# Other periods for the sums, steps and loads of one kv batch in a pipelined attention and adapter kernel

## The chip, the cores and the metric

The kernel runs on one core of one Trainium2 chip. The metric is the device time of an execution in microseconds (us). Before the change it is 384.3 us, the median of 3 runs (384.18 to 384.46).

## The reference

Four batches of 12288 query tokens attend to a pooled and projected image, and the result goes through a mixture of eight small adapters, of which each token uses two. Cut to what is computed:

```python
# q (4, 12288, 128), kv (4, 384, 32, 128), w_sr (128, 128)
kv_pool = kv.reshape(B, H // 4, 4, W // 4, 4, C).mean(axis=(2, 4))
k = v = kv_pool.reshape(B, -1, C) @ w_sr          # 768 keys a batch
a = softmax(q @ k.T / sqrt(C))
x = a @ v                                         # 49152 tokens in all
logits = x @ w_gate                               # 8 experts
topk = the two largest logits of a token; w = softmax over these two
out = x + sum over the two experts e of w_e * ((x @ A[e]) @ B[e])   # rank 16
```

## The kernel before, in words

The 49152 tokens are 96 chunks of 512, 24 to a batch. A hand-written main loop runs over c = 2 to 94, and I call one pass a period. All engines run their instructions in the order in which this loop records them; nothing reorders them. In one period TensorE does, in this order: two groups of scores (L303, keys against queries, each group two matmuls into one of two score banks), with the first half of the weighing of chunk c-1 (L315, values against exps) between them; from c=10 on the up projection of an older chunk (L462); the second half of the weighing; a kv step if one is due in this period (prep_step); the turn of the normalised x of chunk c-2 (t_ps, L381); a third group of scores; and from c=9 on the hidden matmul of an older chunk (L416). At the end of the periods 6 and 8 a further group of scores is recorded, so that scores run a little further ahead.

ScalarE takes the exp of each score group (L304), and in odd periods, between the second and the third exp, the tanh of the gates of a pair of chunks (L358). It also copies the results of the kv steps out of the score banks (L191, L199, L207). VectorE normalises (L322, L326), finds the largest logits (L333), and does the other evacuations. GpSimd computes the arguments of the gates for a pair of chunks in even periods (gate, L342 to L346, behind VectorE's L333), casts the next queries to f16 (cast_q, L107), and sums the kv rows. SyncE issues the loads, the turns of the queries by DMA (L114), the transport of the gates (L402, L409) and the stores.

While the loop works on one batch, the keys and values of the next are prepared. A batch has three tiles of kv, each loaded in four rows of 512 KB (load_row, L87). sum_row (L173) adds row d to row 0 on GpSimd, three times a tile, and after the third sum_cols (L177, L178) halves the row twice. Then TensorE has three steps a tile, in three periods: pooled_transposed (kp_ps, L189) in period k, values (v_ps, L197) in k+2, keys (k_ps, L205) in k+3. Each writes to a score bank that ScalarE copies out. The keys of the second batch are first used by the scores at the end of c=22.

When this happens stands in three lists in plan(b): `at` gives the periods of the 12 loads, `sm` those of the 9 row sums, `st` those of the three first steps. For the second batch, b=1, the numbers are periods themselves; for later batches they are relative to the period at which the batch before begins. prep, called near the end of each period behind gate and cast_q, issues the loads and the sums that are due; so in an even period a sum stands behind that period's gate and cast, and in an odd one it follows what is there. prep_step records a step between the weighing and the turn of x.

In the periods 17, 19 and 21 GpSimd also squares the values (squares, L241 and L245), for a check of ranges.

Of the kernel before, what the change touches and what calls it, by code (L numbers as in the profile page):

```python
# [21 lines left out]
def kernel(  # L22
# [232 lines left out]
    def plan(b):  # L255
        c0 = CPB * (b - 1)
        if b == 1:
            at = [2, 2, 3, 4, 5, 6, 6, 8, 9, 10, 10, 12]
            sm = [5, 5, 7, 9, 9, 11, 13, 13, 15]
            st = [10, 14, 18]  # L260
        else:
            at = [-11, -9, -7, -5, -5, -3, -1, 1, 1, 3, 5, 7]
            sm = [-3, -1, 1, 3, 5, 7, 9, 11, 13]
            st = [4, 10, 16]
        for i, k in enumerate(at):
            loads.setdefault(c0 + k, []).append((b, i // 4, i % 4))
        for i, k in enumerate(sm):
            sums.setdefault(c0 + k, []).append((b, i // 3, i % 3 + 1))
        for t, k in enumerate(st):
            steps[c0 + k] = (pooled_transposed, b, t)  # L270
            steps[c0 + k + 2] = (values, b, t)
            steps[c0 + k + 3] = (keys, b, t)

    for b in range(1, B):
        plan(b)
# [729 lines left out]
```

## Time and profile before

| | us |
|---|---|
| median of 3 runs | 384.3 |
| lowest, highest | 384.18, 384.46 |
| the profiled execution | 383.93 |
| its span in the profile | 382.1 |
| TensorE busy in the span | 363.3 |
| ScalarE busy | 311.4 |
| VectorE busy | 305.2 |
| GpSimd busy | 224.0 |

The span is the time between the first and the last recorded instruction; the execution's own time is 1.83 us longer. Busy times come from that one execution. PE is TensorE's matmuls, PEld its weight loads, DVE is VectorE, ACT ScalarE, POOL GpSimd, SP SyncE. In a timeline row the first number is the start in us, the second the length of the group, and a bracket at the end gives idle time before it with what ended it. Matmuls are pipelined and the lengths of neighbouring groups overlap, so the pace is read from starts.

### The profile page before, as it was taken

To read this page: it belongs to the slowest core of one execution; us is meant where nothing else is said; L and a number is where in the kernel's file an instruction comes from. 1 tells how busy PE (TensorE), PEld (TensorE's weight loads), DVE (VectorE), ACT (ScalarE), POOL (GpSimd) and SP (SyncE) were. 2 spreads that over 40 slices of the span, in tenths; PEclk is the share of its full clock that TensorE was granted. 3 is DMA by queue.
4 is the path that set the end of the run, shared out by engine and by line. 5 is a ranking of instruction groups with operands and counts; after the bars stand their busy time and mean duration, and the time that the engine had idled before them with its cause. 6 is when DMAs were issued, how large, how long until landed. Compare 5 with 4: busy or idle time off the path is not lost.

```text
span 382.1 us, 10633 instructions
## 1 busy us (share of the span) xinstructions
PE 363.3 (95%) x3962; PEld 268.5 (70%) x3963; DVE 305.2 (80%) x955; ACT 311.4 (82%) x393; POOL 224.0 (59%) x369
## 2 busy tenths in 40 slices
PE   4889999999999999999999999999999999999983
PEld 2457667777777877777777777777776777776772
DVE  3786538787888888888888888888888888889995
ACT  1548998889888988988898899888798798888752
POOL 1012699996889787755679697754443243341253
PEclk9999999999999999999999999999999999999996
DMA  8996999999999999999999999996997898964225
GB/s 254 405 352 193 262 308 235 340 251 330 343 300 320 311 257 320 270 325 296 314 306 307 294 283 329 289 227 183 238 254 224 255 226 194 239 171 146 88 84 195
DMA packets 93466, 100.48 MB, mean 263 GB/s; under 512 B 56676, under 2 KB 56932, under 8 KB 93412
## 3 DMA queue, kind: packets, MB, share of 16 engines
q1 hardware_dynamic: 91940, 99.58, 94.9%
q8 instruction: 31, 0.51, 0.6%
q10 hardware_dynamic: 1472, 0.20, 0.3%
q14 instruction: 23, 0.19, 0.1%
HBM read 62.33 MB, written 25.90 MB: 231 GB/s over the span
## 4 chain that ended last, share of the span: by engine, by line
PE 73%; POOL 10%; DVE 7%; ACT 5%; issue 2%; DMA 2%; SPq 0%; POOLq 0%; DVEq 0%
PE xps L315 29%; PE sg L303 26%; PE d_ps L462 5%; PE t_ps L381 4%; PE h_ps L416 4%; POOL kvt L173 4%; ACT tt L304 4%; DMA kvt<-in_kv_dram 2%; POOL q L107 1%; DVE xn L326 1%; POOL kvt L177 1%; DVE ht L419 1%; PE v_ps L197 1%; POOL msk L345 1%; PE w_ps L584 1%
## 5 line engine op out<-in xcount | busy, mean ns | idle before, releaser
L304 ACT ACTIVATE tt<-sg 128x1024 f16<-128x1024 f32 x288 | 277.5, 1022 | 36.0 <-PE sg L303 35.1
L303 PE MATMUL sg<-qT,kfT 128*128 128x512 f16 x576 | 170.0, 379 | 2.4 <-ACT tt L304 1.6
L315 PEld LDWEIGHTS <-tt 128*128 128x128 f16 x2304 | 148.0, 98 | 27.0 <-DVE xn L326 17.2
L315 PE MATMUL xps<-vext,tt 128*128 128x137 f16 x2256 | 166.3, 223 | 0.0
L476 DVE TENSOR_TENSOR osb<-d_ps,xn 128x512 f32<-128x512 f32 x88 | 60.6, 691 | 32.3 <-PE d_ps L462 32.1
L342 POOL TENSOR_TENSOR arg<-xn,top 128x64 f32<-128x64 f32 x47 | 14.7, 312 | 109.2 <-DVE top L333 93.2
L326 DVE TENSOR_TENSOR xn<-xps,rinv_all 128x548 f32<-128x548 f32 x94 | 68.5, 728 | 3.3
L303 PEld LDWEIGHTS <-kfT 128*128 128x128 f16 x576 | 49.3, 98 | 26.9 <-issue 3.8
L173 POOL TENSOR_TENSOR kvt<-kvt 128x1024 f32<-128x1024 f32 x27 | 63.7, 2359 | 0.2
L419 DVE SCALAR_TENSOR_TENSOR ht<-ge,h_ps 128x512 bf16<-128x512 f16 x90 | 60.5, 672 | 2.9 <-PE h_ps L416 2.4
L107 POOL CAST q<-q 128x1024 f16<-128x1024 f32 x44 | 45.6, 1036 | 24.9 <-DMA q<-in_q_dram 24.9
L462 PEld LDWEIGHTS <-ht 128*128 128x128 bf16 x368 | 27.3, 97 | 24.7 <-DVE ht L419 3.7
L333 DVE MAX8 top<-xn 128x8 f32<-128x8 f32 x376 | 35.2, 156 | 6.3
L392 DVE COPY xt<-t_ps 128x512 bf16<-128x512 bf16 x92 | 36.7, 399 | 0.0
L381 PE MATMUL t_ps<-id_bf,xn 128*128 128x128 bf16 x376 | 36.3, 219 | 0.0
L416 PE MATMUL h_ps<-xt,a_bf 128*128 128x512 bf16 x89 | 33.7, 379 | 1.0 <-ACT tt L304 0.7
L462 PE MATMUL d_ps<-b_bf,ht 128*128 128x128 bf16 x352 | 33.6, 219 | 0.9 <-ACT tt L304 0.7
L322 DVE RECIPROCAL rinv_all<-xps 128x4 f32<-128x4 f32 x94 | 17.1, 182 | 15.4 <-PE xps L315 13.1
L381 PEld LDWEIGHTS <-xn 128*128 128x128 bf16 x376 | 26.0, 98 | 0.3
L345 POOL TENSOR_SCALAR msk<-msk 128x64 f32<-128x64 f32 x47 | 20.1, 428 | 4.1
L346 POOL TENSOR_TENSOR arg<-arg,msk 128x64 f32<-128x64 f32 x47 | 15.0, 319 | 3.9
L344 POOL TENSOR_TENSOR arg<-arg,msk 128x64 f32<-128x64 f32 x47 | 15.0, 319 | 3.7
(151 smaller groups left out, 228.4 us busy)
## 6 DMA issues: line engine op xcount, KB each, us to landing
kvt<-in_kv_dram SPq DMA_DIRECT2D x48, 512.0 KB
q<-in_q_dram SPq DMA_DIRECT2D x44, 512.0 KB
out_dram<-osb SPq DMA_DIRECT2D x44, 512.0 KB
ge<-g_h SPq DMA_DIRECT2D x45, 256.0 KB
q<-in_q_dram SPq DMA_DIRECT2D x2, 1024.0 KB
out_dram<-osb SPq DMA_DIRECT2D x8, 256.0 KB
g_h<-g_sb SPq DMA_DIRECT2D x45, 16.0 KB
qT<-q SPq DMA_TRANSPOSE x44
```

Of the source, the lines that this page charges most:

```text
L107: nc.gpsimd.tensor_copy(q16[i], q32[i].rearrange("p k n -> p (k n)"))
L173: eng.tensor_tensor(v[:, 0], v[:, 0], v[:, d], op=ALU.add)
L303: mm(sg[:, k], kfT[b][:, j * P:(j + 1) * P], qc, start=True, stop=True)
L304: nc.scalar.activation(tt[c][:, 2 * r:2 * r + 2], sg, AF.Exp, bias=0.0, scale=scale)
L315: mm(o, tt[c][:, j, s * P:(s + 1) * P], vext[b][:, j, 0:VW], start=(j == 0 and s % 2 == 0), stop=(j == NJ - 1 and s % 2 == 1), skip_group_ ...
L326: nc.vector.tensor_tensor(xn[c].rearrange("p (b s) v -> p b s v", b=2), xv, ri.rearrange("p (b s) -> p b s", b=2).unsqueeze(3).broadcast_t ...
L381: mm(columns(t_ps, c, s), src[:, s], id_bf, is_transpose=True, start=(s == 0), stop=(s == NS - 1), skip_group_check=True)
L392: nc.vector.tensor_copy(to, t_ps)
L416: mm(h_ps, a_bf, xT[c], start=True, stop=True)
L419: nc.vector.scalar_tensor_tensor(hgT[c].rearrange("p (k a) t -> p k (a t)", k=2), gE[c // 2][:, h:h + NS // 2].rearrange("p a t k -> p k ( ...
L462: mm(dps[c][:, s], columns(hgT[c], c, s), b_bf, start=(s == 0 and fresh), stop=(s == NS - 1), skip_group_check=True)
L476: nc.vector.tensor_tensor(osb[:, lo:hi], d, xn[c][:, lo:hi, 0:C], op=ALU.add)
```

## The change

Only the lists for the second batch change, and with them the places of 12 loads, 9 row sums, 3 pairs of column sums and 9 steps. The lists of the later batches stay as they are.

```diff
         if b == 1:
-            at = [2, 2, 3, 4, 5, 6, 6, 8, 9, 10, 10, 12]
-            sm = [5, 5, 7, 9, 9, 11, 13, 13, 15]
-            st = [10, 14, 18]
+            at = [2, 2, 3, 4, 5, 5, 6, 8, 9, 9, 11, 13]
+            sm = [3, 5, 6, 8, 9, 10, 12, 14, 16]
+            st = [9, 13, 18]
```

By tile, the sums go from the periods 5, 5, 7 to 3, 5, 6, from 9, 9, 11 to 8, 9, 10 and from 13, 13, 15 to 12, 14, 16, the column sums with the last of each three. The steps pooled, values and keys go from 10, 12, 13 to 9, 11, 12, from 14, 16, 17 to 13, 15, 16, and stay at 18, 20, 21 for the third tile. Four loads move: the second row of the second tile from 6 to 5, and of the third tile the second row from 10 to 9, the third from 10 to 11 and the fourth from 12 to 13.

## The prediction

> **What bounds the kernel now.** Periods are numbered by the loop variable c. Each holds one t_ps group on TensorE (the turn of x, L381), so I use its start as the mark of a period; it is 61.35 us for c=10 and 91.47 us for c=18. I read first the page's chain of work that ended last, then GpSimd's timeline, then TensorE stage by stage between those marks, then what ScalarE waited for. The page:
>
> ```profile
> span 382.1 us, 10633 instructions
> ...
> PE 73%; POOL 10%; DVE 7%; ACT 5%; issue 2%; DMA 2%; SPq 0%; POOLq 0%; DVEq 0%
> ...
> L173 POOL TENSOR_TENSOR kvt<-kvt 128x1024 f32<-128x1024 f32 x27 | 63.7, 2359 | 0.2
> ```
>
> TensorE owns 73% of the chain, but GpSimd owns a tenth, and the kv sums (L173, 2.36 us each, with 0.2 us of waiting before all 27 of them) are in it. The chain's pieces of GpSimd lie between 41.5 and 88 us, in the plan that is changed. GpSimd's timeline there (start, length):
>
> ```profile
> 44.35 4.78 POOL L173 TENSOR_TENSOR kvt<-kvt 128x1024 f32<-128x1024 f32 x2
> 49.10 0.30 POOL L342 TENSOR_TENSOR arg<-xn,top 128x64 f32<-128x64 f32 x1
> ...
> 50.66 0.32 POOL L346 TENSOR_TENSOR arg<-arg,msk 128x64 f32<-128x64 f32 x1
> ...
> 55.70 0.72 POOL L178 TENSOR_TENSOR kvt<-kvt 128x256 f32<-128x256 f32 x1
> 56.39 0.31 POOL L342 TENSOR_TENSOR arg<-xn,top 128x64 f32<-128x64 f32 x1
> ...
> 65.55 0.32 POOL L346 TENSOR_TENSOR arg<-arg,msk 128x64 f32<-128x64 f32 x1
> ...
> 86.18 0.30 POOL L342 TENSOR_TENSOR arg<-xn,top 128x64 f32<-128x64 f32 x1
> ...
> 89.00 1.24 POOL L241 TENSOR_TENSOR sq<-vext 128x272 f32<-128x272 f16 x2
> 92.95 0.31 POOL L342 TENSOR_TENSOR arg<-xn,top 128x64 f32<-128x64 f32 x1 [2.71 <-DVE top L333]
> ```
>
> From 44.35 us to the gate at 86.18 us (c=16) there is no idle time in these rows: a gate takes over as the last sum ends (55.70 + 0.72 is 56.42, the gate starts at 56.39). At 92.95 us (c=18) GpSimd waits for VectorE again, as it should. Two lengths serve below: gate start to gate end is 50.66 + 0.32 - 49.10 = 1.88 us, and gate start over cast, one sum and both column sums is 56.42 - 49.10 = **7.32 us**.
>
> What this lateness costs is read on TensorE, mark to mark (us, then PE, PEld, DVE, ACT, POOL busy, clock, DMA share, GB/s):
>
> ```profile
> 57.73:61.35 3.62, 3.57 (x43) 2.78 (x42) 3.01 (x11) 3.60 (x5) 3.54 (x4) 1.00 0.81 248
> 61.35:64.75 3.40, 3.40 (x42) 2.57 (x39) 2.70 (x9) 3.05 (x5) 3.24 (x5) 1.00 1.21 330
> 64.75:69.07 4.32, 4.07 (x46) 3.10 (x44) 3.44 (x13) 3.40 (x5) 4.15 (x5) 1.00 1.04 242
> 69.07:72.58 3.51, 3.51 (x43) 2.68 (x41) 2.66 (x8) 3.05 (x4) 3.19 (x7) 1.00 1.05 396
> 72.58:76.59 4.01, 3.83 (x44) 2.81 (x42) 3.07 (x12) 3.55 (x6) 3.85 (x5) 1.00 1.25 269
> ...
> 83.96:87.47 3.51, 3.51 (x43) 2.68 (x41) 2.66 (x8) 3.05 (x4) 3.19 (x7) 1.00 0.87 287
> 87.47:91.47 4.00, 3.83 (x44) 2.81 (x42) 3.06 (x12) 3.54 (x6) 2.69 (x5) 1.00 1.27 283
> 91.47:94.87 3.40, 3.40 (x41) 2.56 (x39) 2.71 (x9) 3.05 (x5) 1.67 (x6) 1.00 1.00 340
> ```
>
> A period without a kv step is 3.40 us. The steps lie just ahead of t_ps, and TensorE's timeline gives their start, and the marks 83.96, 87.47 and 91.47 above their end:
>
> ```profile
> 83.45 0.68 PE L197 MATMUL v_ps<-wext,kp_keep 128*128 128x136 f32 x4
> ...
> 87.36 0.28 PE L205 MATMUL k_ps<-id_h,vext 128*128 128x128 f16 x2
> ...
> 91.25 0.38 PE L189 MATMUL kp_ps<-id_f,kvt 128*128 128x128 f32 x2
> ```
>
> Values (L197) cost 0.51, keys 0.11, the pooled turn 0.22 us. So the excess over work is 4.32 - 3.40 - 0.51 = 0.41 (c=12), 4.01 - 3.62 = 0.39 (c=14) and 4.00 - 3.62 = 0.38 us (c=18): **1.18 us**, and nothing in the other rows. Its cause is on ScalarE, in its timeline and its waits from 33 to 110 us:
>
> ```profile
> 65.91 0.32 ACT L358 ACTIVATE gw_all<-arg 128x64 f16<-128x64 f32 x1 [0.82 <-DVE xn L326]
> ```
>
> ```profile
> ACT gw_all L358 <- POOL arg L346: 2.0, 5, 0.5
> ```
>
> The tanh at 65.91 follows GpSimd's row 65.55 + 0.32 = 65.87 directly, so that wait is GpSimd's too (the label is the view's guess). ScalarE would have taken this tanh at 65.91 - 0.82 = 65.09, 3.74 us after its gate's mark 61.35. It stands in line ahead of the exps and of the key copy, and TensorE waits for those.
>
> Behind 91.47 us TensorE alone sets the pace (its busy row, then all it waited for in these 253 us):
>
> ```profile
> 91.47:345.00 253.53, 252.39 (x2852) 189.29 (x2850) 215.25 (x694) 220.92 (x272) 159.36 (x263) 1.00 1.04 273
> ```
>
> ```profile
> PE h_ps L416 <- ACT tt L304: 0.7, 3, 0.2
> PE d_ps L462 <- ACT tt L304: 0.5, 2, 0.2
> ```
>
> So whatever this plan gains or loses by c=18 stands in the total, one for one: there is no later wait to swallow it.
>
> **The change part by part.** No instruction is added or removed; twelve loads, nine row sums with their column sums, and nine steps move. VectorE's order is the same.
>
> *Sums.* One 2.36 us sum goes to c=3, ahead of the stretch without idle time, and the third tile's last sum with its columns goes from 15 to 16. GpSimd has no gate in odd periods, so the sums of 8 and 9 still follow each other without a gate between, as 9 and 9 did. A gate is on time when it ends by 3.74 us behind its mark, so when it starts by 3.74 - 1.88 = 1.86 us behind it. That of c=10 started at 65.87 - 1.88 = 63.99, 0.8 too late; with 2.36 us less ahead it starts with its data. What VectorE needs is in the rows of c=18: weighing done at 91.25, gate at 92.95, 1.70 us.
>
> *Loads.* A sum at c=3 is safe if its two loads (issued in c=2) have landed by about 38.2 us:
>
> ```profile
> 37.00:38.00 1.00, 1.00 (x9) 0.31 (x6) 0.93 (x3) 0.97 (x3) 1.00 (x2) 1.00 0.00 0
> ...
> 39.00:43.00 4.00, 4.00 (x49) 2.96 (x48) 1.61 (x7) 3.77 (x5) 1.32 (x4) 1.00 1.04 288
> ```
>
> ```profile
> 38.69 0.53 SPq L87 DMA_DIRECT2D kvt<-in_kv_dram  x1
> ```
>
> The DMA is silent from 37 to 38, so they have. The tightest is then the load of c=3 (38.69), needed at 44.35: 5.7 us. Ahead of it stand one q load and itself, 1.05 MB, and 4 us at 288 GB/s carry 1.15 MB, so it lands about 43. The others have two to three periods. SyncE's queue gets one issue more (0.5 to 0.7 us) ahead of the gates' transfers in 5, 9 and 13; these are used periods later. I take nothing. If a load were late, GpSimd's gate and cast queued behind the sum would be late as well, by at most what the load lacks; that falls inside the slow end below.
>
> *Steps 9, 11, 12.* The pooled turn comes in c=9, where ScalarE is still behind from the extra score issued at c=8. Its timeline shows the copy that goes with a pooled turn:
>
> ```profile
> 61.55 0.38 ACT L191 ACTIVATE kp_keep<-kp_ps 128x256 f32<-128x256 f32 x1
> ```
>
> In c=9 it could push the exps, so it costs between 0 and 0.4; I take 0: the step brings 0.22 us of TensorE's own, and the tanh in line ahead of the copy is no longer held up.
>
> *The walk.* Mark of 9: 57.73 + 0.22 = 57.95. 10: + 3.40 = 61.35. 11 (values): + 3.91 = 65.26. 12 (keys): + 3.51 = 68.77. 13 (pooled): + 3.62 = 72.39. 14: 75.79. 15 (values): 79.70. 16 (keys): 83.21. The gates keep up: that of 10 at 61.35 + 1.70 = 63.05, then 7.32 us with sum and columns to 70.37, in time for c=12 (68.77 + 1.86 = 70.63); behind 12 and 14 stands one sum each, and GpSimd idles. Then two bare periods: TensorE stands at the third pooled turn of c=18 at 83.21 + 6.80 = **90.01 us**. Before, it stood there at 91.25 us. The 0.41 and 0.39 are gone by here (keys now fall on even periods, where no tanh is), and 0.38 with them; that would be a gain of 1.2 us.
>
> *The third tile.* That turn reads the tile that GpSimd sums in c=16. GpSimd's order there is gate, cast, sum, two column sums, with nothing to take out. Its gate starts 1.70 us after the weighing ends, so at 83.21 - 0.11 + 1.70 = 84.80, and the columns end 7.32 us later, at **92.12 us**. From a mark to the turn two periods on TensorE needs 6.80 us, GpSimd about 8.9. Before, the sum stood in c=15, right behind the gate of 14, and the turn at 91.25 found it done at about 86.2. Now TensorE waits 92.12 - 90.01 = 2.11 us. Queued behind it are the turn of x, the third score, the hidden matmul, and through them ScalarE's exps. The squares behind the columns (1.24 us) and the gate of 18 fall inside this wait. From here the orders are the same, so the end is late by 92.12 - 91.25 = **+0.9 us**: 2.1 lost, 1.2 won.
>
> The profiled execution took 383.93 us for a span of 382.1; it would be 384.8. Beside the median of the runs, 384.3, that is 385.2.
>
> Ends: if none of the 0.80 us ahead of c=16 is won, everything there is 0.8 later and the loss is 1.7; with the copy of c=9 alone, 1.3; if the tanh waits that left no excess on TensorE win 0.3 as well, 0.6. The forecast's own range is 384.9 to 386.0.
>
> **The rivals.**
>
> *The clock falls in the wait.* The trace has one case of a wait like this one, on TensorE near the end:
>
> ```profile
> 375.20 0.40 PE L762 MATMUL e<-id_bf,hgs 128*128 128x128 bf16 x4 [1.92 <-DVE hgs L753]
> ```
>
> ```profile
> 374.00:376.00 2.00, 0.80 (x7) 0.81 (x8) 1.83 (x6) 1.51 (x4) 0.90 (x2) 0.87 0.59 227
> 376.00:378.00 2.00, 2.00 (x17) 1.48 (x16) 0.85 (x3) 0.91 (x3) 1.09 (x4) 0.50 0.68 262
> ```
>
> After 1.92 us of waiting the granted clock went to 0.50. What a cold start costs is in the warming matmuls:
>
> ```profile
> 6.04 6.12 PE L584 MATMUL w_ps<-id_bf 128*128 128x512 bf16 x18 [0.26 <-DVE vext L168]
> ...
> 19.13 1.89 PE L584 MATMUL w_ps<-id_bf 128*128 128x512 bf16 x8
> ```
>
> Eight warm ones take 1.89 us, so 18 would take 4.25 at most, and the first 18 took 6.12: 1.9 us lost. That gives 385.2 + 1.9 = 387.1. Against it: at 375 other short waits came first, here TensorE is full on both sides. The Trainium skill (TensorE: Matmul & The Clock Gate, "Why this matters for your kernels") asks for no gap over some 3 us between bursts; by that rule 2.1 us leave the clock alone and the time is the forecast's. The row at 375.20 shows a fall after less, so I don't rest on it.
>
> *A larger gain ahead of it.* TensorE waited at both extra scores:
>
> ```profile
> 47.98 0.59 PE L303 MATMUL sg<-qT,kfT 128*128 128x512 f16 x2 [0.66 <-ACT tt L304]
> 55.43 0.59 PE L303 MATMUL sg<-qT,kfT 128*128 128x512 f16 x2 [0.72 <-ACT tt L304]
> ```
>
> I hold these for the cost of two extra exps through two score banks. If they too came from late gates, 1.38 us more is won, ahead of c=16: 385.2 - 1.4 = 383.8, within 0.2%. Against: only one tanh before them waited, and the exps around them run back to back.
>
> *The wait does not bind.* If the columns of c=16 end by 90.0 us, TensorE never waits and only the 1.2 us gain is left: 384.3 - 1.2 = **383.1**. It decides at GpSimd's chain: 7.32 us would have to be 5.2, or the two periods 8.9 us long. For it: spans on GpSimd are rough, and no wait of TensorE for GpSimd stands in the trace of before. Against: gate to gate, that chain repeats to within 0.1 us.
>
> *It does not do what it says* would be a first sum held up by its load; the silent DMA speaks against it, and its time lies on the slow side of the forecast's range.
>
> **How the numbers follow.** A difference under 0.2% (0.77 us) can't be told from no change here. Forecast 385.2 us: chance 0.60, of which 0.44 over 385.07 and 0.16 under. Clock: 0.14, slower. Larger gain: 0.11, same. No wait: 0.15, faster. So slower 0.58, same 0.27, faster 0.15. The range of 383.7 to 387.3 us holds all but the last rival and a little at its ends.
>
> **What would show it.** Right: TensorE's turn of the third tile (L189) at c=18 preceded by about 2 us of waiting for L178 on GpSimd; no tanh (L358) waiting for L346 between 55 and 88 us; periods of 3.40 plus their step from 10 to 17. Wrong: that turn without a wait; the waits of 0.66 and 0.72 gone; the clock under 1 at 92 us; GpSimd waiting for a load ahead of a sum.

## The result, and the profile after

The changed kernel takes **386.71 us** (median of 6 executions, 385.02 to 387.28) against 384.06 for the kernel before in the same comparison (383.33 to 384.46): 1.006 times as long, with an interval of 1.0035 to 1.0086. Two of the six lie at 385.0 to 385.1 us, the profiled one (385.12, span 383.3) among them; four lie at 386.4 to 387.3. Two further sets of twelve have medians of 386.24 and 385.82 against 384.11 and 384.17. So the profile after shows a loss of 1.2 us, and the medians of the three sets lie 1.7 to 2.7 us above those of the kernel before. Both have to be explained. The kernel before has a spread too: its 99 executions beside the experiments below reach from 383.37 to 387.96 us.

The page of the profile after:

```profile
span 383.3 us, 10632 instructions
...
PE 82%; DVE 6%; ACT 5%; POOL 2%; DMA 2%; issue 1%; SPq 0%; DVEq 0%; POOLq 0%; ACTq 0%
```

GpSimd's share of the chain fell from 10% to 2%: the lateness that the change was to lift is lifted, and the time still grew. TensorE from mark to mark (the start of t_ps, as in the prediction), periods 10 to 19:

```profile
58.11:61.68 3.57, 3.51 (x41) 2.61 (x39) 2.80 (x10) 3.37 (x6) 3.49 (x3) 1.00 1.22 238
61.68:65.59 3.91, 3.91 (x46) 3.06 (x44) 3.35 (x12) 3.40 (x5) 3.23 (x7) 1.00 1.03 397
65.59:69.10 3.51, 3.51 (x43) 2.68 (x41) 2.71 (x9) 3.08 (x5) 3.43 (x3) 1.00 1.17 239
69.10:72.77 3.67, 3.67 (x44) 2.82 (x42) 2.98 (x11) 3.35 (x5) 3.34 (x8) 1.00 1.05 383
72.77:76.17 3.40, 3.40 (x41) 2.57 (x39) 2.80 (x10) 3.15 (x6) 3.10 (x2) 1.00 1.27 182
76.17:80.08 3.91, 3.91 (x46) 3.07 (x44) 3.34 (x12) 3.39 (x5) 1.97 (x6) 1.00 1.05 403
80.08:83.59 3.51, 3.51 (x43) 2.68 (x41) 2.71 (x9) 3.08 (x5) 2.98 (x2) 1.00 1.61 211
83.59:87.04 3.45, 3.45 (x42) 2.60 (x40) 2.78 (x10) 3.12 (x5) 1.61 (x6) 1.00 0.78 255
87.04:92.85 5.81, 3.84 (x45) 2.82 (x43) 4.45 (x17) 3.43 (x5) 5.65 (x6) 1.00 1.18 293
92.85:96.24 3.39, 3.39 (x41) 2.56 (x39) 1.54 (x3) 2.92 (x4) 3.14 (x8) 1.00 1.04 402
```

Where before there were 4.32, 4.01 and 4.00 us, every period up to 17 is now its bare 3.40 plus its step, to within 0.17 us. Then one period takes 5.81. TensorE's timeline and GpSimd's show why:

```profile
92.57 0.44 PE L189 MATMUL kp_ps<-id_f,kvt 128*128 128x128 f32 x2 [1.97 <-POOL kvt L178]
92.85 0.39 PE L381 MATMUL t_ps<-id_bf,xn 128*128 128x128 bf16 x4
```

```profile
85.18 0.31 POOL L342 TENSOR_TENSOR arg<-xn,top 128x64 f32<-128x64 f32 x1 [2.12 <-DVE top L333]
...
88.01 2.36 POOL L173 TENSOR_TENSOR kvt<-kvt 128x1024 f32<-128x1024 f32 x1
...
91.80 0.72 POOL L178 TENSOR_TENSOR kvt<-kvt 128x256 f32<-128x256 f32 x1
92.47 1.24 POOL L241 TENSOR_TENSOR sq<-vext 128x272 f32<-128x272 f16 x2
```

The gate of c=16 is on time (GpSimd even waits 2.12 us for it), the columns end 91.80 + 0.72 - 85.18 = 7.34 us later, and TensorE has been waiting at the third pooled turn for 1.97 us.

Executions begin up to 1.4 us apart (the mark of c=8 lies between 53.18 and 54.58 us in the traces of this study), so traces are compared below from the mark of c=8 to that of c=25. Before it is 62.59 us, after 63.81: **+1.22**. The two rows:

```profile
53.44:116.03 62.59, 61.22 (x687) 46.21 (x686) 48.83 (x159) 55.23 (x70) 54.44 (x78) 1.00 1.12 301
```

```profile
53.60:117.41 63.81, 61.06 (x686) 46.23 (x685) 48.87 (x159) 55.02 (x70) 53.25 (x77) 1.00 1.10 306
```

### The profile page after: what moved, and what is told of

It reads as the page before. It is cut to its first block, busy times and chain, and to the rows that moved or that the text cites. A ratio compares the mean times of both kernels' runs of the same rounds, so it can differ in the third digit from the quotient of the medians.

```text
span 383.3 us, 10632 instructions
## 1 busy us (share of the span) xinstructions
PE 362.2 (94%) x3962; PEld 268.0 (70%) x3963; DVE 305.1 (80%) x955; ACT 311.4 (81%) x393; POOL 224.2 (58%) x369
## 4 chain that ended last, share of the span: by engine, by line
PE 82%; DVE 6%; ACT 5%; POOL 2%; DMA 2%; issue 1%; SPq 0%; DVEq 0%; POOLq 0%; ACTq 0%
PE xps L315 33%; PE sg L303 29%; PE d_ps L462 5%; PE t_ps L381 5%; PE h_ps L416 4%; ACT tt L304 4%; DMA kvt<-in_kv_dram 2%; PE v_ps L197 1%; DVE xn L326 1%; DVE ht L419 1%; PE w_ps L584 1%; DVE osb L476 1%; DVE kvt L173 1%; POOL kvt L173 1%; PE kp_ps L189 1%
```

## The experiments

The theory: (a) the earlier sums and steps of the first two tiles win about 1 us, (b) the wait of TensorE for the third tile's column sums costs 2 us in every execution, (c) in part of the executions the granted clock falls behind that wait and costs about 2 us more. Rivals: another moved piece makes the loss (loads, squares); the spread comes from somewhere else. In the expectations, "slow group" means the longer ones among the executions of one kernel. The ratios are to the kernel before, run beside each set of four rows: 384.11 us (first four), 384.08 (second four) and 384.17 us (last four). The last column is taken from one trace each.

| kernel | median us | lowest, highest | ratio, 95% | mark 8 to 25, us |
|---|---|---|---|---|
| changed, again | 386.24 | 384.93, 389.19 | 1.0022 to 1.0078 | 65.48 |
| steps at 19 | 384.14 | 383.22, 385.08 | 0.9967 to 1.0008 | 62.96 |
| before, last sum at 16 | 385.27 | 384.63, 386.71 | 0.9997 to 1.0041 | 63.94 |
| sum ahead of the cast | 384.70 | 383.84, 388.05 | 0.9976 to 1.0034 | 62.82 |
| steps at 17 | 391.36 | 390.91, 391.81 | 1.0155 to 1.0216 | 69.13 |
| idle matmuls in the wait | 385.09 | 384.26, 386.23 | 1.001 to 1.0042 | 63.79 |
| sums at 13 and 15 | 384.20 | 383.14, 385.61 | 0.998 to 1.0014 | 62.19 |
| before, new loads only | 385.18 | 383.79, 386.64 | 1.0006 to 1.0042 | 63.15 |
| changed, beside the next three | 385.82 | 384.46, 387.14 | 1.0009 to 1.0054 | 63.80 |
| idle matmuls, beside | 385.65 | 384.85, 387.39 | 1.0017 to 1.0056 | 63.79 |
| sums at 13, 15, loads at 10, 12 | **383.06** | 382.28, 383.89 | 0.995 to 0.9986 | 61.63 |
| steps at 19, squares later | 384.90 | 384.07, 385.66 | 0.9999 to 1.0034 | 61.82 |

**The changed kernel once more** (no edit).

> The changed kernel once more, for its spread and a second trace. Its six executions so far lie in two groups, 385.0 to 385.1 us (the profiled one among them) and 386.4 to 387.3 us; the kernel before lies between 383.3 and 384.5. Theory: the 2 us wait of TensorE ahead of the third pooled turn (L189, c=18) costs about 1 us net in every execution, and in most of them the granted clock falls to 0.5 behind that wait and costs about 2 us more. Then the runs show both groups again, and a trace of the slow group shows a clock of 0.5 for some 3 us just behind 92.6 us and the same period lengths as before elsewhere. Rival: the slow group comes from somewhere else (the end of the kernel, a late transfer); then a slow trace has full clock at 92 us and its loss at another place.

This trace is of one of the longer executions, 386.51 us. The wait at the third turn is the same (1.98 us), but behind it the next period takes 97.92 - 92.86 = 5.06 us where it took 3.39. Its stages, with the granted clock as the third number from the end:

```profile
92.00:93.00 1.00, 0.42 (x5) 0.41 (x6) 0.00 (x0) 0.00 (x0) 1.00 (x2) 1.00 1.17 359
93.00:94.00 1.00, 1.00 (x9) 0.48 (x7) 0.07 (x1) 0.67 (x2) 1.00 (x4) 0.92 1.01 373
94.00:95.00 1.00, 1.00 (x7) 0.69 (x6) 0.96 (x2) 1.00 (x2) 0.83 (x3) 0.50 1.16 453
95.00:96.00 1.00, 1.00 (x11) 1.00 (x9) 0.00 (x0) 0.73 (x1) 0.92 (x3) 0.50 0.95 393
96.00:97.00 1.00, 1.00 (x6) 0.45 (x4) 0.00 (x0) 0.00 (x0) 1.00 (x2) 0.50 1.06 329
97.00:98.00 1.00, 1.00 (x18) 1.00 (x16) 0.63 (x1) 1.00 (x2) 0.92 (x2) 0.87 1.28 203
```

The clock is at half from about 93.8 to 97.3 us (0.92 and 0.87 are the shares of the first and the last of these), and the period is 5.06 - 3.39 = **1.67 us** longer. The rest up to mark 25 is as in the profile after: 65.48 - 63.81 = 1.67. So up to there the longer of these two executions is longer by the clock and nothing else (over the whole it is 1.39 us longer, as the clock falls later at its end, at 384.0 us for 377.4). This is (c), and the rival of a loss elsewhere is out for this execution. The two groups of the first six did not come again: the twelve spread from 384.93 to 389.19 us. And the mean granted clock of this execution is 0.995, in spite of the fall.

**The third tile's steps a period later.**

```diff
-            st = [9, 13, 18]
+            st = [9, 13, 19]
```

> The changed kernel with the third tile's steps one period later (19, 21, 22 for 18, 20, 21). TensorE comes to the turn at about 94 us, the column sums end at about 92.5, so the wait of 1.97 us goes. Theory: both the net loss and the slow group go, and what is left is the gain of the earlier part, 0.8 us by the changed trace (the turn of c=18 could start at 90.6 - 0.17 where it started at 91.25 before): 383.2 us, with a spread as small as that of before. Rival, that the loss comes from the other moved sums and loads: it stays near 386. Rival, that the early sums gain nothing: 384.1.

The wait at the turn is gone, and so are the executions above 385.1 us. But the time is that of before, 384.14, and not 383.2. TensorE's mark 18 lies at 90.02, 36.84 us behind mark 8 where before, without its 0.22 us of step, it was 37.81: the gain of (a) is there, **0.97 us**. It is lost again, and 0.37 us more in this trace, in the next two periods. ScalarE's waits from 80 to 100 us:

```profile
ACT gw_all L358 <- POOL arg L346: 1.5, 1, 1.5
```

GpSimd has the squares of c=17 behind the column sums, and only then the gate of c=18, which comes 1.4 us late; the tanh waits, the pooled copy behind it too, and TensorE loses 1.2 us at 95.86. In the changed kernel the wait at the turn had covered this. So the theory was right on the wait and wrong on what is left without it.

**One number in the kernel before.**

```diff
-            sm = [5, 5, 7, 9, 9, 11, 13, 13, 15]
+            sm = [5, 5, 7, 9, 9, 11, 13, 13, 16]
```

> The kernel before with one number changed: the last sum (with the column sums) in period 16 for 15. Theory: the gate of c=16 then starts with its data at about 85.1, the columns end 7.3 us later at 92.5, and TensorE, which comes to the turn at about 90.9, waits 1.6 us: net 1.2 us later than before in every execution, 385.3, and some executions 2 us slower still by the clock. Rival, that other moves of the change make the loss: 384.1, no wait.

TensorE waits 1.47 us for L178, and the median is 385.27, 1.16 us over before (the interval of the ratio just holds 1). The trace has +1.35. So this one move makes a loss of the size seen after, without the others. The executions "2 us slower still by the clock" did not come: the lowest mean clock is 0.991, and the trace has no fall at the turn. Here (b) alone is seen.

**The sum ahead of the cast in c=16.**

```diff
             gate(c // 2 - 1, nc.gpsimd)
+            if c == 16:
+                prep(c)
             if c // 2 + 4 < 2 * NQ:
                 cast_q(c // 2 + 4)
...
-        prep(c)
+        if c != 16:
+            prep(c)
```

> The changed kernel with the sum and the column sums of period 16 recorded ahead of the cast of that period on GpSimd, so that the columns end 1.0 us earlier. Theory: the wait shrinks from 1.97 to about 1.0 us, the profiled span by 1.0 us, and 1 us of waiting is too short for the clock to fall: 384.1 us with one group of runs. Rival, that the slow group has another cause: two groups again, about 1 us lower each. Rival, that the fall of the clock does not depend on the length of the wait: the same.

The wait is 0.99 us and the trace 62.82, 0.99 under the profile after: the cast's microsecond comes back in full. The median, 384.70, is less clear than that, 0.6 us over the 384.1 expected. One execution took 388.05 us, with a mean clock of 0.987. No trace shows where its clock fell, so that a wait of 1 us is too short for a fall is not shown.

**The steps a period earlier.**

```diff
-            st = [9, 13, 18]
+            st = [9, 13, 17]
```

> The changed kernel with the third tile's steps one period earlier (17, 19, 20 for 18, 20, 21). TensorE comes to the turn at about 87.2 us and the column sums end at about 92.5, so the wait grows from 1.97 to about 5.4 us, and the turn of x of c=18 comes at 96.2 where it came at 92.85: 3.4 us later, 388.4 us at full clock. Theory, that the clock falls when a wait is long beside some 3.4 us: it falls in every execution, for some 3.4 us, and costs 1.4 to 1.9 us more: about 390, in one group. Rival, that the slow group has another cause: two groups as before, 388.4 and 390.3.

The wait is 5.36 us and the clock is at half from within the wait on:

```profile
90.00:92.00 2.00, 0.00 (x0) 0.00 (x0) 0.00 (x0) 0.00 (x0) 1.88 (x2) 0.92 1.18 123
92.00:94.00 2.00, 1.84 (x9) 1.23 (x10) 0.00 (x0) 0.38 (x1) 1.30 (x3) 0.50 0.72 234
94.00:96.00 2.00, 2.00 (x17) 1.19 (x16) 1.12 (x3) 1.68 (x2) 0.00 (x0) 0.73 1.04 414
```

All four executions lie together, from 390.9 to 391.8, which fits a fall in each of them; but four are few, and only one was traced. The expected 390 was 1.4 short, of which 0.5 us is a new wait at c=24.

**Idle matmuls in the wait.** Seven matmuls whose results nothing reads, ahead of the turn of c=18.

```diff
     def prep_step(c):
+        if c == 18:
+            warm(7)
         if c in steps:
```

> The changed kernel with 7 idle matmuls (1.5 us, results unused) on TensorE ahead of the third pooled turn, so that TensorE works during most of the wait for GpSimd while the turn comes no sooner. Theory, wait and clock: the wait shrinks to some 0.4 us, the turn of x still comes where it came, the net loss of about 1.1 us stays, and the slow group is gone: 385.2 us, all executions within about 0.7 us. Rival, that the slow group is not the clock: the median stays at 386.2 to 386.7 with two groups.

TensorE now works through most of the wait, and the turn comes no sooner:

```profile
90.37 1.67 PE L586 MATMUL w_ps<-id_bf 128*128 128x512 bf16 x7
92.28 0.44 PE L189 MATMUL kp_ps<-id_f,kvt 128*128 128x128 f32 x2 [0.24 <-POOL kvt L178]
```

The trace is 63.79 us, as after. The median is 385.09, but the executions spread over 2 us, more than expected. Beside the changed kernel on one chip, with that kernel again:

> The changed kernel on the same chip as the next three, for comparison. Theory: executions from about 385 us up, those with a fall of the clock behind the third turn 1.4 to 2 us above; median 386.2 to 386.7 as in both sets so far.

> Again the changed kernel with 7 idle matmuls ahead of the third pooled turn, now beside the changed kernel itself. Theory, that half of the loss is the clock: the median is 1.0 to 1.5 us under that of the changed kernel of the same call, about 385.1, and still 1 us over before. Rival, that the difference between the two was that of two chips: less than 0.4 us between them.

The medians, 385.82 and 385.65, differ by 0.17 us and the means, 385.75 and 385.66, by 0.09, where 1.0 to 1.5 was expected and the rival said less than 0.4. So in time this comparison does not show (c), and the size of (c) stays open. Over all executions the means are 386.19 us (30 of the changed kernel) and 385.40 (24 with idle matmuls), but these come in part from different chips.

What speaks for (c) is the clock. A mean granted clock of 0.990 or less comes in 9 of the 30 executions of the changed kernel, in none of the 24 with idle matmuls (lowest 0.991, which the fall at the kernel's end alone gives, as in the profile of before), and in 5 of the 99 of the kernel before. Those 5 took 386.2 to 388.0 us with no such wait, so some long executions have another cause, which no trace here shows. The measure also misses falls: the two traced executions with a fall at the third turn have means of 0.995 and, with the steps at 17, 0.991. The loss without a fall is clearer: the 5 executions of the changed kernel with a mean clock of 0.999 or more average 385.20 us and the 23 of the kernel before 384.10, a difference of 1.1 us.

The traces also suggest why the same wait is followed by a fall in one execution and not in another. In all 14 traces each stretch of full clock that ends in a fall is a whole multiple of 3.413 us long (81.92 us is 24 times that, 365.23 us 107 times), counted from the clock's first rise, which lies between 8.8 and 12.5 us. So the clock falls only on a beat, and the beat lies elsewhere in each execution. In the trace with the fall the beat from 90.43 to 93.84 us holds the whole wait, and TensorE is busy for 1.43 us of it. In the other two traces of the changed kernel the beats that hold most of the wait have 1.54 us (90.70 to 94.11) and 1.91 us of work (90.98 to 94.39), and no fall follows. Three traces do not settle where the limit lies: at the end of the next kernel, with its sums at 13 and 15, a fall follows a beat with 1.64 us of work.

**The third tile's sums earlier.**

```diff
-            sm = [3, 5, 6, 8, 9, 10, 12, 14, 16]
+            sm = [3, 5, 6, 8, 9, 10, 12, 13, 15]
```

> The changed kernel with the third tile's second and third sum one period earlier (12, 13, 15 for 12, 14, 16), all else as changed. By the changed trace the gate of c=14 starts at about 78.2 (0.3 behind its data, due by 78.0), the third sum and the columns end by about 85.6, and the gate of 16 is due by 85.45. Theory: no wait at the turn, no late gate of c=18 behind squares as in the run with steps at 19, so the gain of the earlier part stands: 0.8 to 1.2 us under before, 383.0 to 383.3 us, below both kernels. Rival, that the early sums gain nothing: 384.1.

There is no wait at the turn, but only 0.40 us is won in the trace, and the median is 0.1 us over that of the kernel before. GpSimd's timeline names the reason, a load:

```profile
82.30 2.36 POOL L173 TENSOR_TENSOR kvt<-kvt 128x1024 f32<-128x1024 f32 x1 [0.76 <-DMA kvt<-in_kv_dram]
```

**The new loads in the kernel before.**

```diff
-            at = [2, 2, 3, 4, 5, 6, 6, 8, 9, 10, 10, 12]
+            at = [2, 2, 3, 4, 5, 5, 6, 8, 9, 9, 11, 13]
```

> The kernel before with only the list of the loads changed. Theory: no sum waits for a load in either trace, so nothing changes: 384.1 us. Rival, that the moved loads delay other transfers: slower by more than 0.3 us.

The same load holds up the third sum, by 0.50 us; the gate behind it comes later, and TensorE loses 0.71 us where it lost 0.17 (the key copy of c=17). The trace has +0.56, the median +1.10. So the theory missed here: the loads do matter where the sum stands at 15. In the changed kernel it stands at 16, and no sum waits for a load.

**Both mended.** Sums at 13 and 15 with the third tile's last loads at 10 and 12.

```diff
-            at = [2, 2, 3, 4, 5, 5, 6, 8, 9, 9, 11, 13]
-            sm = [3, 5, 6, 8, 9, 10, 12, 14, 16]
+            at = [2, 2, 3, 4, 5, 5, 6, 8, 9, 9, 10, 12]
+            sm = [3, 5, 6, 8, 9, 10, 12, 13, 15]
```

> The kernel with third-tile sums in 12, 13 and 15, and now also its last two loads in 10 and 12, as before the change, instead of 11 and 13. In the run with the later loads the sum of c=15 waited 0.76 us for a load issued at c=13, and the gate of 16 behind it held up a tanh by 0.95 us and TensorE by 0.39 us. Theory: with the load a period sooner that wait goes, and c=18 comes some 0.4 to 0.5 us sooner than there: mark 8 to mark 25 in 61.75 us against 62.59 of before, and 383.3 us in all, 0.8 under before. Rival, that the load lands late whatever its period: 384.2 as there.

This kernel beats both: **383.06 us**, 0.997 times before (0.995 to 0.9986), and its trace has 0.96 us less from mark 8 to mark 25. The periods 17 to 19 have no excess left:

```profile
83.31:86.77 3.46, 3.46 (x43) 2.61 (x41) 2.79 (x10) 3.14 (x5) 3.21 (x6) 1.00 1.04 388
86.77:90.38 3.61, 3.61 (x44) 2.77 (x42) 3.17 (x12) 3.42 (x5) 2.59 (x5) 1.00 1.22 241
90.38:93.78 3.40, 3.40 (x41) 2.57 (x39) 2.71 (x9) 3.05 (x5) 1.67 (x6) 1.00 1.04 372
```

**The steps later, and the squares out of the way.**

```diff
-        if k in (17, 19, 21) and b + 1 < B:
-            if b == 0:
-                squares(0, (k - 17) // 2)
-            squares(b + 1, (k - 17) // 2)
+        if b == 0 and k in (18, 20, 22):
+            squares(0, (k - 18) // 2)
+            squares(1, (k - 18) // 2)
+        elif b and k in (17, 19, 21) and b + 1 < B:
+            squares(b + 1, (k - 17) // 2)
```

> The changed kernel with steps at 19, 21, 22, and the first squares one period later (18, 20, 22), so that they stand behind the gate of 18 and not ahead of it. With the steps alone moved, that gate came 1.4 us late behind column sums and squares, and TensorE waited 1.2 us for ScalarE at c=19 to 20. Theory: that wait goes, and the gain of the earlier part is left: mark 8 to mark 25 in about 61.8 us against 62.59, and 383.3 us. Rival, that the squares do not matter: 384.1 as with the steps alone.

Mark 25 comes 61.82 us behind mark 8, as expected, and the wait at 18 to 20 is gone. But the median is 384.90, and the trace shows one reason: the last squares now stand at c=22, with a sum of the third batch behind them, and the gate of c=24 is late in turn. ScalarE's timeline:

```profile
117.60 0.32 ACT L358 ACTIVATE gw_all<-arg 128x64 f16<-128x64 f32 x1 [1.76 <-POOL arg L346]
```

TensorE loses 1.20 us at 118.88 us, just behind the stretch that I had compared.

## Why the prediction was right, point by point

*The bound.* Right. The three excesses of 0.41, 0.39 and 0.38 us were late gates: in the profile after no tanh waits for GpSimd between 33 and 110 us, and the excesses are gone. The key copies moved to even periods at the same time, and no run moves the sums alone, so how the gain divides between sums and steps is not shown.

*The walk.* Right in every step to within 0.2 us. Against mark 8, TensorE stood at the third turn 0.97 us sooner than before where 1.24 was worked out. The missing 0.27 is the period of c=10, 3.57 for 3.40 (the pooled turn in c=9, taken as nothing with 0.4 as its other end), and 0.05 us each at 13 and 17. It was not the copy on ScalarE that cost it, as the prediction feared: in the profile after the third score group of c=9 starts at 58.51 us, just behind the end of an exp at 58.46, where before it started at 57.96 with that exp running to 58.29, and the copy comes only at 58.56. The pooled turn holds one of the two score banks, so the likely reason is that the score had to wait for the other.

*The third tile.* Right: gate 1.70 us behind the weighing, 7.34 us to the end of the columns where 7.32 was taken, and a wait of 1.97 us by the view where 2.11 was said. The view counts from the modelled end of the weighing; from the start that the turn would have had, 87.04 + 3.40, it is 92.57 - 90.44 = 2.13. The run with one number changed in the kernel before shows such a wait (1.47 us) without the rest.

*The sum.* The profiled execution was put at 384.8 us and took 385.12; 0.22 us of the difference is the walk up to the gate of c=16. As a forecast of the executions on the whole, 385.2 us was low, by 1.5 us against the median of the first six and by 0.9 against that of all 30. The measured 386.71 lies over the forecast's own range of 384.9 to 386.0; it is inside the wide range only because the rival of the clock had stretched that to 387.3. So the way and the wait were foreseen, and that the number fits so far is in part luck.

*The clock.* This step failed, in its chance. It stood as a rival with 0.14 at 387.1 us, but it does not stand against the forecast's wait; it can follow it. The wait is there in all three traces of the changed kernel, the fall behind it in one. In how many executions it comes is not shown; a low mean clock in 9 of 30 against 5 of 99 before says that it is a part of them. I argued that TensorE is full on both sides; the fall came all the same. The row at 375.20, a fall behind 1.92 us of waiting and some shorter waits, had shown that it can. The price of 1.9 us was near the 1.67 measured. The Trainium skill (TensorE: Matmul & The Clock Gate, "Why this matters for your kernels") asks for no gap over some 3 us. The trace of the changed kernel run again does not bear that out as a safe limit: there 1.98 us was enough.

*The larger gain, and no wait.* Neither came: the waits at the extra scores stayed (1.4 us in two, as before), and the turn did wait.

*The loads.* "I take nothing" held for the kernel as changed. As a statement on those loads it was too easy: the trace of before shows no load late, but the one moved to c=13 landed some 6 us behind its issue, and a sum at 15 finds it missing.

## What to carry to other kernels

When work moves in a hand-made schedule, follow each consumer with the chain of its producer: here two periods of TensorE, 6.8 us, were set against 7.3 us of GpSimd that could not begin before the gate's data, 1.7 us in. A queue without slack hands a delay on, to the squares, the gate and the load in turn, and only the version that made room for all of them has a median clear of the kernel before. And a wait of TensorE can cost its own length in one execution and a fall of the clock besides in the next, which one profile does not show: look at the spread and the granted clock of the executions, and at those of the kernel before as well.

## What the runs showed of the hardware

Behind a single wait of 2.0 us between stretches in which TensorE is full, the granted clock fell to 0.50 in one of three traces of the changed kernel, and stayed there for 3.4 us of dense work. With 5.4 us of waiting it fell in the one execution traced, within the wait. With 1.7 us of idle matmuls in the wait it fell there in neither of two traces. In all 14 traces it fell only at whole multiples of 3.413 us behind its first rise, and that rise lies elsewhere in each execution. The mean granted clock was 0.990 or less in 9 of 30 executions with the 2.0 us wait, in 0 of 24 with idle matmuls in it, and in 5 of 99 of the kernel before, which waits nowhere near the third turn for more than 0.17 us.
